# Retention, low-rank mixing and MLP on one core: q, k, v loaded as float32 by SP's queue in a fixed order, and mixing that ends at nine tenths of the MLP beside it

## The chip, the cores and the metric

One core of one Trainium2 chip. The metric is device time in microseconds (us). Most runs of one kernel agree within about 1%. The record marks each run as fast or slow. The medians here are over all runs. The traces are of one profiled execution each. A trace's span is about 2 us shorter than the time of its run, and can differ by more from the median where slow runs are in it.

The engines are TensorE (PE in the profile), VectorE (DVE), ScalarE (ACT), GpSimd (POOL) and SyncE (SP), which here only issues DMA transfers. The granted clock is the share of TensorE's full clock that the chip allowed.

## The reference, cut to what matters

```python
# q, k, v: (8, 8, 576, 64) float32
scores = scale * q @ k^T                          # per batch and head
ret = scores * gamma**(i - j) for i >= j          # causal decay
x = (ret @ v), heads side by side: (8, 576, 512)
h = (x^T @ U @ V)^T                               # mixing over the sequence, rank 32
u = x + h
out = u + max(u @ w_ch1, 0) @ w_ch2               # MLP, 512 -> 2048 -> 512
```

## The kernel before

Two batches are packed into nine chunks of 128 rows. Chunks 0 to 4 make an "A" group (its MLP covers 4 chunks), chunks 5 to 8 a "B" group (its MLP covers 5, since chunk 4 is shared). There are eight groups. While TensorE works through the MLP of group g ("main"), the attention and mixing of group g+1 ("fill") are woven between its matmuls, and the loads of group g+2 are under way.

```python
def interleave(main, fill, lead=0.0, end=1.0):    # fill spread over lead..end of main
    ...

def load_chunk(p, c, cast_dma):
    t = qkv_pool.tile([P, 3, H, D], BF16, tag="qkv", name="qkv")
    if cast_dma:                                  # groups 2 to 7
        for j, dram in ((1, k), (0, q), (2, v)):
            for rows, b, t0 in parts(p, c):
                nc.gpsimd.dma_start(out=t[rows, j, :, :], in_=dram[...])   # f32 -> bf16
        scale_v(t, t, p, c)                       # POOL: v times decay
        return t
    ...                                           # groups 0 and 1: f32 by nc.sync

def attention_items(p, chunks, st, pe_transpose, lag):
    def T(c):                                     # q, k to qkT, crossbar transpose
        nc.sync.dma_start_transpose(out=qkT, in_=t[:, 0:2, :, :]...)
    def SC(c):                                    # scores into psc
        ...
        if c == XC:                               # the shared chunk
            nc.gpsimd.tensor_copy(out=qT[:, :, 0:HALF], in_=qkT[...])      # qTx, POOL
        ...
        nc.vector.tensor_tensor(out=ret, in0=psc, in1=mask, op=ALU.mult)   # DVE
    def RV(c):                                    # ret @ v into po, then xt on DVE
        ...

def mixer_items(p, par, st, pe_transpose):
    def MT(c):                                    # u to uT, input of the next MLP
        nc.sync.dma_start_transpose(out=dst, in_=st["u", c])
    ...

with tc.manual_schedule(engines={PE, POOL}):      # these two in program order
    ...
    for g, (p, par) in enumerate(groups):
        if g + 2 < len(groups):
            load_group(*groups[g + 2])
        fill = front_items(*groups[g + 1]) if g + 1 < len(groups) else []
        interleave(mlp_items(p, par, sts[p]), fill, 0.35 if g == 0 else 0.0)
```

TensorE and POOL run in program order. The order of the other engines, and of SP's DMA queue, is chosen by the scheduler at compile time. Each engine then executes its own list strictly in order.

Of the kernel before, what the change touches and what calls it, by code (L numbers as in the profile page):

```python
# [12 lines left out]
ALU = mybir.AluOpType  # L13
PE = mybir.EngineType.PE
POOL = mybir.EngineType.Pool


def interleave(main, fill, lead=0.0, end=1.0):


    tm = sum(c for c, _ in main) or 1
    tf = sum(c for c, _ in fill) or 1
    i = j = 0
    dm = df = 0.0
    while i < len(main) or j < len(fill):
        if j >= len(fill) or (
            i < len(main) and dm / tm <= lead + (end - lead) * df / tf
        ):
            dm += main[i][0]
            main[i][1]()  # L30
            i += 1
        else:
            df += fill[j][0]
            fill[j][1]()
            j += 1
# [3 lines left out]
def kernel(  # L39
# [11 lines left out]
    nc = tc.nc  # L51

    B, H, S, D = q.shape
# [3 lines left out]
    P = 128  # L57
    HALF = 64
# [7 lines left out]
    XC = 4  # L66
# [31 lines left out]
    vscale = consts.tile([P, NCH, H], FP32, name="vscale")  # L98
# [7 lines left out]
    vx = [consts.tile([P, H, D], BF16, name=f"vx{i}") for i in range(2)]  # L106
# [67 lines left out]
    def parts(p, c):  # L174

        if c < XC:
            return [(slice(0, P), 2 * p, c * P)]
        if c > XC:
            return [(slice(0, P), 2 * p + 1, c * P - 4 * P - HALF)]
        return [(slice(0, HALF), 2 * p, 4 * P), (slice(HALF, P), 2 * p + 1, 0)]  # L180

    def scale_v(t, f, p, c):
        nc.gpsimd.tensor_tensor(  # L183
            out=t[:, 2, :, :], in0=f[:, 2, :, :],
            in1=vscale[:, c, :, None].to_broadcast([P, H, D]), op=ALU.mult,
        )
        if c == XC:
            nc.gpsimd.tensor_copy(out=vx[p % 2][HALF:P, :, :], in_=t[HALF:P, 2, :, :])


    def load_chunk(p, c, cast_dma):
        t = qkv_pool.tile([P, 3, H, D], BF16, tag="qkv", name="qkv")
        if cast_dma:
            for j, dram in ((1, k), (0, q), (2, v)):
                for rows, b, t0 in parts(p, c):
                    L = rows.stop - rows.start
                    nc.gpsimd.dma_start(  # L197
                        out=t[rows, j, :, :],
                        in_=dram[b, :, t0:t0 + L, :].rearrange("h s d -> s h d"),
                    )  # L200
            scale_v(t, t, p, c)
            return t
        f = stage.tile([P, 3, H, D], FP32, tag="stage", name="stage_t")
        for j, dram in ((1, k), (0, q), (2, v)):
            for rows, b, t0 in parts(p, c):
                L = rows.stop - rows.start
                nc.sync.dma_start(  # L207
                    out=f[rows, j, :, :],
                    in_=dram[b, :, t0:t0 + L, :].rearrange("h s d -> s h d"),
                )  # L210
        nc.vector.tensor_copy(out=t[:, 0:2, :, :], in_=f[:, 0:2, :, :])  # L211
        scale_v(t, f, p, c)
        return t


    def attention_items(p, chunks, st, pe_transpose, lag):
        items = []
        qkv = st["qkv"]

        def T(c):  # L220
            t = qkv[c]
# [98 lines left out]
        def add(fn, c, w):  # L320
            items.append((w, lambda: fn(c)))
# [9 lines left out]
        n = len(chunks)  # L331
        if chunks[0] == XC + 1:
            add(ST, XC, 230)
        for s in range(n + lag):
            if s < n:
                add(T, chunks[s], 460 if pe_transpose else 0)
            if lag and s >= lag:
                add(RV, chunks[s - lag], 232)
            if s < n:
                c = chunks[s]  # L340
                if c not in (XC, NCH - 1):
                    add(ST, c, 230)
                add(SC, c, 520)
                if not lag:
                    if c > 0:
                        add(MA0, c - 1, 216)
                    add(RV, c, 232)
        if not lag:
            add(MA0, chunks[-1], 216)
        return items  # L350


    def mixer_items(p, par, st, pe_transpose):
        items = []
        Ub, Vb = (U_A, V_A) if par == 0 else (U_B, V_B)
        c0 = 0 if par == 0 else XC

        def MA(i):
            if pe_transpose:
                pass  # L360
            elif i == 0:
                st["a"] = ps_s.tile([P, dm], FP32, tag="ps_s", name="psa")
            if not pe_transpose:
                nc.tensor.matmul(  # L364
                    st["a"], Ub[:, i, :], st["x", c0 + i], start=(i == 0), stop=(i == 4),
                )
            if i == 4:
                a_sb = mix_pool.tile([P, dm], BF16, tag=f"a_sb{par}", name="a_sb")
                nc.scalar.activation(out=a_sb, in_=st["a"], func=AF.Copy)  # L369
                st["a_sb", par] = a_sb  # L370

        def MH(c):
            if c % 2 == 0:
                ph = ps_s.tile([P, dm], FP32, tag="ps_s", name="ph")
            else:
                ph = ps_o.tile([P, 2, 512], FP32, tag="ps_o", name="ph")[:, 0, :]
            i = c - c0
            if c == XC:
                nc.tensor.matmul(
                    ph, V_A[:, 4 * P:5 * P], st["a_sb", 0], start=True, stop=False  # L380
                )
            nc.tensor.matmul(  # L382
                ph, Vb[:, i * P:(i + 1) * P], st["a_sb", par],
                start=(c != XC), stop=True,
            )
            ut = u_pool.tile([P, dm], BF16, tag="u", name="ut")
            st["u", c] = ut
            nc.vector.tensor_tensor(out=ut, in0=ph, in1=st["x", c], op=ALU.add)  # L388

        def MT(c):  # L390
            dst = st["uT", par][:, :, (c - c0) * P:(c - c0 + 1) * P]
            if not pe_transpose:
                nc.sync.dma_start_transpose(out=dst, in_=st["u", c])  # L393
                return
            pu = ps_big.tile([P, NCC, P], BF16, tag="ps_big", name="pu")
            for cc in range(NCC):
                nc.tensor.transpose(
                    pu[:, cc, :], st["u", c][:, cc * P:(cc + 1) * P], ident
                )
            nc.scalar.activation(out=dst, in_=pu, func=AF.Copy)  # L400

        def start():
            n = 4 if par == 0 else 5
            st["uT", par] = uT_pool.tile([P, NCC, n * P], BF16, tag=f"uT{par}", name="uT")

        for i in range(5):
            items.append((216, lambda i=i: MA(i)))
        items.append((0, start))
        for c in range(c0, c0 + (4 if par == 0 else 5)):
            items.append((216, lambda c=c: MH(c)))  # L410
            items.append((230 if pe_transpose else 0, lambda c=c: MT(c)))
        return items
# [48 lines left out]
    NP = B // 2  # L461
    sts = [{"qkv": {}} for _ in range(NP)]
    A_CH = list(range(0, XC + 1))
    B_CH = list(range(XC + 1, NCH))

    def load_group(p, par, cast_dma=True):
        for c in A_CH if par == 0 else B_CH:
            sts[p]["qkv"][c] = load_chunk(p, c, cast_dma)

    def front_items(p, par, pe_t=False, lag=1):  # L470
        st = sts[p]
        return attention_items(
            p, A_CH if par == 0 else B_CH, st, pe_t, lag
        ) + mixer_items(p, par, st, pe_t)

    with tc.manual_schedule(engines={PE, POOL}):
        early_consts()
        for c in A_CH:
            sts[0]["qkv"][c] = load_chunk(0, c, False)
            if c == 1:  # L480
                load_mixer()
            if c == 3:
                load_w1([0])
        interleave([], front_items(0, 0, True, 0))
        load_w1(range(1, dff // W1B))
        load_w2()
        load_group(0, 1, False)
        groups = [(p, par) for p in range(NP) for par in range(2)]
        for g, (p, par) in enumerate(groups):
            if g + 2 < len(groups):  # L490
                load_group(*groups[g + 2])
            fill = front_items(*groups[g + 1]) if g + 1 < len(groups) else []
            interleave(mlp_items(p, par, sts[p]), fill, 0.35 if g == 0 else 0.0)


# [28 lines left out]
```

## Time and profile before

| | before |
|---|---|
| median of 3 runs | 409.43 us (408.39 to 411.16) |
| span of the trace | 410.2 us |
| first MLP matmul | 42.2 us |
| mean granted TensorE clock | 0.929 |
| length of the eight groups, us | 66.1, 47.5, 40.2, 46.2, 38.9, 51.2, 37.0, 41.0 |

The length of a group runs from its first MLP matmul to the next group's first, in the timeline of TensorE; the last one runs to the end of the span. The page, engines and DMA queues (packets, megabytes, share of 16 engines):

```profile
PE 329.0 (80%) x2406; PEld 179.1 (44%) x2440; DVE 126.0 (31%) x172; ACT 123.5 (30%) x244; POOL 137.4 (33%) x176
...
q0 software_dynamic: 90176, 14.97, 49.1%
q1 hardware_dynamic: 83456, 28.85, 35.2%
```

TensorE leads, but is idle for a fifth of the span. Where it waits, in the view of waits (total us, times, longest us):

```profile
PE ps_y_940 L429 <- DMA uT<-ut: 21.0, 1, 21.0
...
PE psc L265 <- DMA qkT<-qkv: 6.1, 1, 6.1
...
PE ps_y_2783 L429 <- DMA uT<-ut: 4.0, 1, 4.0
PE ps_y_1469 L429 <- DMA uT<-ut: 3.5, 1, 3.5
PE ps_y_2383 L429 <- DMA uT<-ut: 3.4, 1, 3.4
```

L429 is the first MLP layer: every joint, the passage from one group to the next, waits for uT, the transposed output of the mixing, and the first joint waits 21 us. The timeline of SP's queue shows why (start us, us, what):

```profile
82.79 1.23 SPq L225 DMA_TRANSPOSE qkT<-qkv  x1
84.12 0.53 SPq L447 DMA_DIRECT2D out_dram<-o_sb  x1
89.93 1.23 SPq L225 DMA_TRANSPOSE qkT<-qkv  x1
91.22 0.57 SPq L447 DMA_DIRECT2D out_dram<-o_sb  x1
97.01 1.23 SPq L225 DMA_TRANSPOSE qkT<-qkv  x1
98.34 0.52 SPq L447 DMA_DIRECT2D out_dram<-o_sb  x1
98.95 5.34 SPq L393 DMA_TRANSPOSE uT<-ut  x4
104.40 0.53 SPq L447 DMA_DIRECT2D out_dram<-o_sb  x1
105.47 1.19 SPq L393 DMA_TRANSPOSE uT<-ut  x1
```

The mixing's matmuls ended at 87.3 us, but the uT transposes (L393) start at 98.95. In front of them stand attention transposes of the third group (L225) at 7.1 us intervals. They wait for POOL's cast loads, whose timeline is:

```profile
76.39 1.04 POOL L183 TENSOR_TENSOR qkv<-qkv,vscale 128x512 bf16<-128x512 bf16 x1 [3.53 <-DMA qkv<-in_v_dram]
77.38 0.94 POOL L197 DMA_DIRECT2D qkv<-in_k_dram  x1
78.31 0.89 POOL L197 DMA_DIRECT2D qkv<-in_q_dram  x1
79.18 0.90 POOL L197 DMA_DIRECT2D qkv<-in_v_dram  x1
83.58 1.04 POOL L183 TENSOR_TENSOR qkv<-qkv,vscale 128x512 bf16<-128x512 bf16 x1 [3.50 <-DMA qkv<-in_v_dram]
```

POOL issues a chunk's three loads, waits 3.5 us for them, scales v, and only then issues the next chunk: 7.2 us per chunk. A long wait also costs clock. The windows view of TensorE (length, busy us, matmuls, granted clock, DMA share, GB/s):

```profile
85.00:90.00 5.00, 2.25 (x10) 0.95 1.40 140
90.00:95.00 5.00, 0.00 (x0) 0.50 0.89 135
...
105.00:110.00 5.00, 1.65 (x8) 0.50 1.65 179
110.00:115.00 5.00, 4.80 (x30) 0.66 1.36 106
```

After the wait the matmuls go on at half clock for some microseconds.

### The profile page before, as it was taken

Reading aid. Unit: us, or ns where it says so; the run is one execution under the profiler, and the core shown is the slowest. Engines: PE = TensorE matmul, PEld = TensorE weight load, DVE = VectorE, ACT = ScalarE, POOL = GpSimd, SP = SyncE. Lnnn points to the kernel's source line nnn. Section 1 sums busy time; section 2 is a strip of 40 time slices with the busy share of each in tenths; the row PEclk is TensorE's granted clock in tenths of the full one; section 3 lists DMA queues with packets and bytes.
Section 4 is the critical chain, followed back from the end, with each engine's and each line's share of the span. In section 5 each row is a group of like instructions: output and inputs, shape, how many; then the busy total and the mean of one; then the engine's idle time right before and its main releaser. Section 6 shows DMA issues by size and latency. Waiting matters only on the chain.

```text
span 410.2 us, 5915 instructions
## 1 busy us (share of the span) xinstructions
PE 329.0 (80%) x2406; PEld 179.1 (44%) x2440; DVE 126.0 (31%) x172; ACT 123.5 (30%) x244; POOL 137.4 (33%) x176
## 2 busy tenths in 40 slices
PE   2554948950499987997899969993999979988995
PEld 1442414420276433543675434541675435435642
DVE  4445003440033341334134323431324323350021
ACT  3222542000166003610572015301571026105700
POOL 2835805457336436533643426333100000000000
PEclk9999987985599996999899989996899989999999
DMA  9999999999999999999999949999120220031011
GB/s 182 202 204 182 205 180 134 95 120 138 149 90 93 100 189 108 91 127 132 126 93 100 144 108 90 102 123 144 27 53 27 88 67 0 27 90 53 0 53 77
DMA packets 173659, 44.19 MB, mean 108 GB/s; under 512 B 164864, under 2 KB 169024, under 8 KB 173632
## 3 DMA queue, kind: packets, MB, share of 16 engines
q0 software_dynamic: 90176, 14.97, 49.1%
q1 hardware_dynamic: 83456, 28.85, 35.2%
q8 instruction: 19, 0.31, 0.3%
q14 instruction: 8, 0.07, 0.1%
HBM read 37.00 MB, written 9.44 MB: 113 GB/s over the span
## 4 chain that ended last, share of the span: by engine, by line
PE 67%; DMA 11%; issue 8%; POOL 7%; SPq 3%; DVE 2%; ACT 1%; POOLq 0%; DVEq 0%
DMA uT<-ut 6%; POOL qkv L197 3%; PE psc L265 3%; POOL qkv L183 2%; DMA w_sb<-in_moe_w_ch_dram 2%; PE po L305 2%; SPq L393 2%; PE psa L364 2%; PE pss L248 1%; POOL w_sb L169 1%; PE ph L382 1%; DMA stage_t<-in_v_dram 1%; DMA U_A<-in_moe_U_dram 1%; SPq L207 1%; PE ps_y_3231 L440 1%
## 5 line engine op out<-in xcount | busy, mean ns | idle before, releaser
L429 PEld LDWEIGHTS <-w_sb 128*128 128x128 bf16 x768 | 74.4, 103 | 96.0 <-issue 38.0
L292 DVE TENSOR_TENSOR ret<-psc,tri 128x1024 bf16<-128x1024 f32 x32 | 39.2, 1224 | 107.9 <-PE psc L265 107.9
L183 POOL TENSOR_TENSOR qkv<-qkv,vscale 128x512 bf16<-128x512 bf16 x27 | 28.0, 1037 | 111.1 <-DMA qkv<-in_v_dram 111.1
L311 DVE TENSOR_TENSOR xt<-po,qscale 128x512 bf16<-128x512 f32 x36 | 24.9, 690 | 53.0 <-PE po L305 53.0
L388 DVE TENSOR_TENSOR ut<-ph,xt 128x512 bf16<-128x512 f32 x36 | 24.8, 690 | 27.1 <-PE ph L382 25.9
L369 ACT ACTIVATE a_sb<-psa 128x512 bf16<-128x512 f32 x8 | 4.8, 597 | 85.8 <-PE psa L364 81.8
L197 POOL DMA_DIRECT2D qkv<-in_k_dram x30 | 26.9, 899 | 7.9 <-PE pss L248 7.9
L197 POOL DMA_DIRECT2D qkv<-in_v_dram x30 | 25.9, 869 | 0.0
L197 POOL DMA_DIRECT2D qkv<-in_q_dram x30 | 25.6, 857 | 0.0
L265 PE MATMUL psc<-qkT 64*128 64x128 bf16 x288 | 16.0, 238 | 9.4 <-DMA qkT<-qkv 6.1
L305 PE MATMUL po<-qkv,ret 128*128 128x64 bf16 x288 | 15.4, 200 | 6.5 <-DVE ret L292 4.6
L255 ACT ACTIVATE s_sb<-pss 128x512 bf16<-128x512 f32 x32 | 19.0, 593 | 4.1 <-PE pss L248 3.9
L305 PEld LDWEIGHTS <-ret 128*128 128x128 bf16 x288 | 13.7, 102 | 12.5 <-DVE ret L292 6.8
L265 PEld LDWEIGHTS <-qkT 64*128 64x128 bf16 x288 | 9.1, 101 | 22.5 <-issue 11.5
L429 PE MATMUL ps_y_940<-uT,w_sb 128*128 128x320 bf16 x4 | 1.2, 459 | 21.0 <-DMA uT<-ut 21.0
L183 POOL TENSOR_TENSOR qkv<-stage_t,vscale 128x512 bf16<-128x512 f32 x9 | 9.3, 1046 | 21.8 <-DMA stage_t<-in_v_dram 17.6
L248 PEld LDWEIGHTS <-qkv 128*128 128x128 bf16 x128 | 11.9, 115 | 8.1 <-issue 3.0
L248 PE MATMUL pss<-qkv 128*128 128x128 bf16 x112 | 13.0, 249 | 1.6 <-ACT s_sb L255 1.0
L211 DVE CAST qkv<-stage_t 128x1024 bf16<-128x1024 f32 x9 | 6.3, 702 | 22.1 <-DMA stage_t<-in_q_dram 22.1
L440 PEld LDWEIGHTS <-y_3632 128*128 128x128 bf16 x80 | 7.8, 98 | 9.3
L440 PEld LDWEIGHTS <-y_2767 128*128 128x128 bf16 x80 | 7.6, 98 | 8.6
L440 PEld LDWEIGHTS <-y_939 128*128 128x128 bf16 x80 | 7.6, 98 | 8.6
(526 smaller groups left out, 568.9 us busy)
## 6 DMA issues: line engine op xcount, KB each, us to landing
out_dram<-o_sb SPq DMA_DIRECT2D x36, 256.0 KB, 2.3
qkv<-in_k_dram POOLq DMA_DIRECT2D x24, 128.0 KB, 3.6
qkv<-in_q_dram POOLq DMA_DIRECT2D x24, 128.0 KB, 4.6
qkv<-in_v_dram POOLq DMA_DIRECT2D x24, 128.0 KB, 4.6
stage_t<-in_k_dram SPq DMA_DIRECT2D x8, 256.0 KB, 5.8
stage_t<-in_q_dram SPq DMA_DIRECT2D x8, 256.0 KB, 5.3
stage_t<-in_v_dram SPq DMA_DIRECT2D x8, 256.0 KB, 5.5
w_sb<-in_moe_w_ch_dram POOLq DMA_DIRECT2D x16, 128.0 KB, 7.0
```

The source lines that it names most:

```text
L183: nc.gpsimd.tensor_tensor(out=t[:, 2, :, :], in0=f[:, 2, :, :], in1=vscale[:, c, :, None].to_broadcast([P, H, D]), op=ALU.mult,)
L197: nc.gpsimd.dma_start(out=t[rows, j, :, :], in_=dram[b, :, t0:t0 + L, :].rearrange("h s d -> s h d"),)
L248: nc.tensor.matmul(pss[:, hp, :], t[:, 1, 2 * hp:2 * hp + 2, :].rearrange("p h d -> p (h d)"), vt[:, 2 * hp:2 * hp + 2, :].rearrange("p h ...
L255: nc.scalar.activation(out=s_sb, in_=pss, func=AF.Copy)
L265: nc.tensor.matmul(psc[:, hl, hp, :], qkT[pb:pb + HALF, NHP + hp, :], qkT[pb:pb + HALF, hp, :], start=True, stop=True,)
L292: nc.vector.tensor_tensor(out=ret.rearrange("p (hp hl) i -> p hl hp i", hl=2), in0=psc, in1=mask[:, None, None, :].to_broadcast([P, 2, NHP ...
L305: nc.tensor.matmul(po[:, hl, hp * D:(hp + 1) * D], ret[:, h, :], t[:, 2, h, :], start=(c == 0 and hp == 0), stop=True, skip_group_check=True,)
L311: nc.vector.tensor_tensor(out=xt.rearrange("p (hp hl d) -> p hl hp d", hl=2, d=D), in0=po[:, :, 0:NHP * D].rearrange("p hl (hp d) -> p hl ...
L364: nc.tensor.matmul(st["a"], Ub[:, i, :], st["x", c0 + i], start=(i == 0), stop=(i == 4),)
L388: nc.vector.tensor_tensor(out=ut, in0=ph, in1=st["x", c], op=ALU.add)
L429: nc.tensor.matmul(ps[:, 0:n], w1_sb[:, cc, f * P:(f + 1) * P], uT[:, cc, t0:t0 + n], start=(cc == 0), stop=(cc == NCC - 1),)
L440: nc.tensor.matmul(ps, st["y1"][:, f, i * P:(i + 1) * P], w2_sb[:, f, :], start=(f == 0), stop=(f == NF - 1),)
```

## The change

Three things are changed together:
- **L, loads.** All q, k, v come as float32 through SP's queue. The cast of q and k moves to DVE. A load can then be issued without POOL.
- **O, order.** SP joins the engines in program order. Each attention transpose is placed one step ahead of its use, each chunk's load after it (before, a group's loads all stood at the start of an MLP).
- **M, mixing.** The fill runs from 0.05 to 0.9 of the MLP in place of 0 to 1, so that uT has time to land.

```diff
-        if cast_dma:
-            ... nc.gpsimd.dma_start(out=t[rows, j, :, :], in_=dram[...])
-            scale_v(t, t, p, c)
-            return t
         f = stage.tile([P, 3, H, D], FP32, tag="stage", name="stage_t")
         ... nc.sync.dma_start(out=f[rows, j, :, :], in_=dram[...])
         nc.vector.tensor_copy(out=t[:, 0:2, :, :], in_=f[:, 0:2, :, :])
...
+        if not pe_transpose:
+            add(T, chunks[0], 0)
         for s in range(n + lag):
-            if s < n:
-                add(T, chunks[s], 460 if pe_transpose else 0)
+            if pe_transpose and s < n:
+                add(T, chunks[s], 460)
+            if not pe_transpose and s + 1 < n:
+                add(T, chunks[s + 1], 0)
+            if loads:
+                items.append((0, lambda a=loads.pop(0): load_chunk(*a)))
...
-    with tc.manual_schedule(engines={PE, POOL}):
+    with tc.manual_schedule(engines={PE, POOL, SPQ}):
...
-            interleave(mlp_items(p, par, sts[p]), fill, 0.35 if g == 0 else 0.0)
+            interleave(main, fill, 0.35 if g == 0 else 0.05, 0.9)
```

More of the change, by code (lines that the diff above doesn't have):

```diff
@@ L15 @@
 POOL = mybir.EngineType.Pool
+SPQ = mybir.EngineType.SP
 def interleave(main, fill, lead=0.0, end=1.0):
@@ L180, in parts, with load_chunk @@
         return [(slice(0, HALF), 2 * p, 4 * P), (slice(HALF, P), 2 * p + 1, 0)]
-    def scale_v(t, f, p, c):
-        nc.gpsimd.tensor_tensor(
-            out=t[:, 2, :, :], in0=f[:, 2, :, :],
-            in1=vscale[:, c, :, None].to_broadcast([P, H, D]), op=ALU.mult,
-        )
-        if c == XC:
-            nc.gpsimd.tensor_copy(out=vx[p % 2][HALF:P, :, :], in_=t[HALF:P, 2, :, :])
-    def load_chunk(p, c, cast_dma):
-        t = qkv_pool.tile([P, 3, H, D], BF16, tag="qkv", name="qkv")
-        if cast_dma:
-            for j, dram in ((1, k), (0, q), (2, v)):
-                for rows, b, t0 in parts(p, c):
-                    L = rows.stop - rows.start
-                    nc.gpsimd.dma_start(
-                        out=t[rows, j, :, :],
-                        in_=dram[b, :, t0:t0 + L, :].rearrange("h s d -> s h d"),
-                    )
-            scale_v(t, t, p, c)
-            return t
+    def load_chunk(p, c):
+        t = qkv_pool.tile([P, 3, H, D], BF16, tag="qkv", name="qkv")
         f = stage.tile([P, 3, H, D], FP32, tag="stage", name="stage_t")
@@ L211, in load_chunk, with attention_items @@
         nc.vector.tensor_copy(out=t[:, 0:2, :, :], in_=f[:, 0:2, :, :])
-        scale_v(t, f, p, c)
-        return t
-    def attention_items(p, chunks, st, pe_transpose, lag):
+        nc.gpsimd.tensor_tensor(
+            out=t[:, 2, :, :], in0=f[:, 2, :, :],
+            in1=vscale[:, c, :, None].to_broadcast([P, H, D]), op=ALU.mult,
+        )
+        if c == XC:
+            nc.gpsimd.tensor_copy(out=vx[p % 2][HALF:P, :, :], in_=t[HALF:P, 2, :, :])
+        sts[p]["qkv"][c] = t
+    def attention_items(p, chunks, st, pe_transpose, lag, loads):
         items = []
         qkv = st["qkv"]
+        loads = list(loads)
         def T(c):
@@ L349, in attention_items @@
             add(MA0, chunks[-1], 216)
+        for a in loads:
+            items.append((0, lambda a=a: load_chunk(*a)))
         return items
@@ L464, with chunks_of, front_items @@
     B_CH = list(range(XC + 1, NCH))
-    def load_group(p, par, cast_dma=True):
-        for c in A_CH if par == 0 else B_CH:
-            sts[p]["qkv"][c] = load_chunk(p, c, cast_dma)
-    def front_items(p, par, pe_t=False, lag=1):
-        st = sts[p]
+    def chunks_of(g):
+        return [(g // 2, c) for c in (A_CH if g % 2 == 0 else B_CH)] if g < 2 * NP else []
+    def front_items(g, loads, pe_t=False, lag=1):
+        p, par = g // 2, g % 2
         return attention_items(
-            p, A_CH if par == 0 else B_CH, st, pe_t, lag
-        ) + mixer_items(p, par, st, pe_t)
-    with tc.manual_schedule(engines={PE, POOL}):
+            p, A_CH if par == 0 else B_CH, sts[p], pe_t, lag, loads
+        ) + mixer_items(p, par, sts[p], pe_t)
+    with tc.manual_schedule(engines={PE, POOL, SPQ}):
         early_consts()
         for c in A_CH:
-            sts[0]["qkv"][c] = load_chunk(0, c, False)
+            load_chunk(0, c)
             if c == 1:
@@ L483 @@
                 load_w1([0])
-        interleave([], front_items(0, 0, True, 0))
+        interleave([], front_items(0, [], True, 0))
         load_w1(range(1, dff // W1B))
         load_w2()
-        load_group(0, 1, False)
-        groups = [(p, par) for p in range(NP) for par in range(2)]
-        for g, (p, par) in enumerate(groups):
-            if g + 2 < len(groups):
-                load_group(*groups[g + 2])
-            fill = front_items(*groups[g + 1]) if g + 1 < len(groups) else []
-            interleave(mlp_items(p, par, sts[p]), fill, 0.35 if g == 0 else 0.0)
+        for a in chunks_of(1):
+            load_chunk(*a)
+        for g in range(2 * NP):
+            main = mlp_items(g // 2, g % 2, sts[g // 2])
+            fill = front_items(g + 1, chunks_of(g + 2)) if g + 1 < 2 * NP else []
+            interleave(main, fill, 0.35 if g == 0 else 0.05, 0.9)
 _INS = ['q', 'k', 'v', 'moe_U', 'moe_V', 'moe_w_ch1', 'moe_w_ch2']
```

## The prediction

> **What bounds the kernel now.** TensorE, with holes. The windows view in 5 us stretches shows it busy nearly 5 of 5 us inside most groups (one MLP of 4 or 5 chunks, with the next group's attention and mixing beside it) and idle at the joints between them. From the first MLP matmul (42 us) to the end I count about 75 us lost:
> - First joint, 87 to 108 us: one wait of 21.0 us for the transposed mixing output (waits view: ps_y_940 on DMA uT). In the SP queue's timeline that transpose stands behind two attention transposes, which wait for cast loads. Those go chunk by chunk: the chain of waits alternates a 1.04 us POOL scale, 2.65 us of issuing and 3.5 us of landing, 7.2 us per chunk.
> - Six later joints: waits of 2.8 to 8 us for uT.
> - After long waits the granted clock falls. The Trainium skill, "TensorE: Matmul & The Clock Gate" (What's actually happening), puts this at about 3.4 us idle. The trace agrees: 0.50 at 155 to 160 us after a gap of 3.5 us, 1.00 after the last joint's waits of 1.3 and 1.9 us. Gaps plus slow clock: about 61 us.
> - In the first group about 9 us, one attention transpose stuck behind weight traffic (psc on qkT, 6.1 us).
>
> **What the change does.** It removes 90 cast issues from POOL (0.87 us each, 78 us), adds 90 hardware issues on SP (0.5 us when free, 1.1 when full, as in the first 20 us) and 27 DVE casts of 0.69 us. POOL scales cost the same; TensorE's work is unchanged. A chunk's load should take 3.6 us (five in 18 us at the start), against 7.2. SP's order is now fixed: uT transposes no longer stand behind later attention transposes, and each attention transpose is queued one step ahead. Mixing ends at 0.9 of the MLP, so 16 matmuls (3.45 us) follow each group's last mixing matmul.
>
> **On the critical path.** The 21 us wait should vanish almost wholly. At other joints, after the last mixing matmul: 1.1 us (DVE), an output issue (0.5), one or two transposes (1.3 each), 3 us from issue to landing; this ends about 2 us after the 3.45 us of matmuls. Each of seven joints keeps about 2 us, mostly too short for the clock to fall: 17 us in place of 61. The first group's hole stays, 3 to 4 us worse: DVE casts the third group's first chunk before the first masking, and that load queues behind two transposes. Loads crowding SP in groups with five loads: 2 us.
>
> 410 - 61 + 17 + 4 + 2: about **371 us**, 8 in 10 between **360** and **387**. Faster by over 2%: 0.96; within 2%: 0.03; slower: 0.01.
>
> **What the profile would show.**
> - Software queue: weights and mixer only; POOL busy near 50 us; DVE near 145.
> - First joint's wait for uT under 4 us; the others 1 to 3; mean clock from 0.93 to 0.96 or more.
> - First MLP matmul still near 42 us; first qkT wait still 6 us or more.
> - After the first group no waits over 2 us for qkT.
>
> **What would make it wrong.** SP is in order: transposes behind three loads in a full queue (one took 10.6 us to issue before) could make TensorE wait for qkT in every group: 385 to 395. DVE is in order too: a cast ahead of a masking, whose load is late, holds TensorE. If uT lands earlier than I count, the joints vanish: 358.

## The result, and the profile after

| | before | changed |
|---|---|---|
| median of 4 runs | 410.3 us | 381.35 us (380.06 to 383.07) |
| ratio | | 0.9289, 95% interval 0.9215 to 0.9363 |
| span of the trace | 410.2 us | 381.3 us |
| first MLP matmul | 42.2 us | 41.8 us |
| mean granted clock | 0.929 | 0.978 |
| groups, us | 66.1, 47.5, 40.2, 46.2, 38.9, 51.2, 37.0, 41.0 | 51.3, 49.9, 35.2, 46.0, 37.1, 45.2, 35.1, 39.8 |

A ratio is the mean time of one kernel's fast runs over that of the other's fast runs of the same rounds, so it is not quite the ratio of the medians. Line numbers move with the edit: L393 of before is L390 here, L225 is L214, L429 is L426.

The page of the changed kernel:

```profile
PE 329.2 (86%) x2440; PEld 176.1 (46%) x2440; DVE 142.9 (37%) x199; ACT 123.2 (32%) x244; POOL 62.4 (16%) x86
...
q1 hardware_dynamic: 167840, 50.09, 73.6%
q0 software_dynamic: 5792, 4.34, 7.5%
```

Waits of TensorE:

```profile
PE po L294 <- DVE ret L281: 9.6, 10, 2.6
...
PE psc L254 <- DMA qkT<-qkv: 5.7, 2, 4.6
...
PE ps_y_936 L426 <- DMA uT<-ut: 1.9, 1, 1.9
PE ps_y_2800 L426 <- DMA uT<-ut: 1.6, 1, 1.6
```

The 21 us are gone. The first joint waits 0.8 and 1.9 us, the other joints 0.6 to 1.6 us. SP's queue at the first joint:

```profile
83.88 0.57 SPq L444 DMA_DIRECT2D out_dram<-o_sb  x1
86.91 2.53 SPq L390 DMA_TRANSPOSE uT<-ut  x2
89.96 0.35 SPq L444 DMA_DIRECT2D out_dram<-o_sb  x1
90.37 3.85 SPq L390 DMA_TRANSPOSE uT<-ut  x3
94.31 0.53 SPq L444 DMA_DIRECT2D out_dram<-o_sb  x1
```

No attention transpose stands in front of uT any more. The saving of 28.9 us (410.2 less 381.3) is unevenly spread. The first group gives 14.9. The third to eighth give 16.0 together, the start 0.4. The second became 2.3 us longer. The new first line of the waits tells of it: TensorE waits for the masking on DVE (ret). Here is DVE in the second group,

```profile
113.79 0.68 DVE L300 TENSOR_TENSOR xt<-po,qscale 128x512 bf16<-128x512 f32 x1
119.22 0.69 DVE L194 CAST qkv<-stage_t 128x1024 bf16<-128x1024 f32 x1 [4.75 <-DMA stage_t<-in_q_dram]
119.83 1.22 DVE L281 TENSOR_TENSOR ret<-psc,tri 128x1024 bf16<-128x1024 f32 x1
```

and TensorE beside it:

```profile
115.89 0.40 PE L254 MATMUL psc<-qkT 64*128 64x128 bf16 x8
...
121.11 0.41 PE L294 MATMUL po<-qkv,ret 128*128 128x64 bf16 x8 [2.64 <-DVE ret L281]
```

The scores were in psc at 116.3 us. DVE could have masked them then, but stood at the cast of a chunk that is needed only in a later group, whose load had not landed. The clock then fell:

```profile
115.00:120.00 5.00, 3.47 (x36) 1.00 1.06 184
120.00:125.00 5.00, 3.89 (x33) 0.72 0.00 0
```

### The profile page after: what moved, and what is told of

Same layout as the page of the kernel before. It is cut to its first block, busy times and chain, and to the rows that moved or that the text cites. A ratio compares the mean times of both kernels' runs of the same rounds, so it can differ in the third digit from the quotient of the medians.

```text
span 381.3 us, 5987 instructions
## 1 busy us (share of the span) xinstructions
PE 329.2 (86%) x2440; PEld 176.1 (46%) x2440; DVE 142.9 (37%) x199; ACT 123.2 (32%) x244; POOL 62.4 (16%) x86
## 3 DMA queue, kind: packets, MB, share of 16 engines
q0 software_dynamic: 5792, 4.34, 7.5%
## 4 chain that ended last, share of the span: by engine, by line
PE 56%; DMA 18%; SPq 13%; DVE 6%; issue 3%; ACT 2%; POOL 1%; DVEq 0%; POOLq 0%
DMA stage_t<-in_q_dram 8%; SPq L190 7%; DMA uT<-ut 4%; SPq L214 4%; DMA stage_t<-in_v_dram 3%; DVE ret L281 3%; PE po L294 2%; PE psc L254 2%; PE psa L361 2%; PE ph L379 1%; SPq L390 1%; DVE o_sb L443 1%; DVE qkv L194 1%; DMA qkT<-qkv 1%; DMA U_A<-in_moe_U_dram 1%
## 5 line engine op out<-in xcount | busy, mean ns | idle before, releaser
L426 PEld LDWEIGHTS <-w_sb 128*128 128x128 bf16 x768 | 72.2, 100 | 55.9 <-issue 17.3
L195 POOL TENSOR_TENSOR qkv<-stage_t,vscale 128x512 bf16<-128x512 f32 x36 | 38.1, 1060 | 216.2 <-DMA stage_t<-in_v_dram 156.0
L194 DVE CAST qkv<-stage_t 128x1024 bf16<-128x1024 f32 x36 | 25.8, 718 | 64.4 <-DMA stage_t<-in_q_dram 64.4
L237 PEld LDWEIGHTS <-qkv 128*128 128x128 bf16 x128 | 10.5, 105 | 6.9 <-issue 1.9
L237 PE MATMUL pss<-qkv 128*128 128x128 bf16 x112 | 12.0, 235 | 1.8 <-ACT s_sb L244 1.0
L437 PEld LDWEIGHTS <-y_3686 128*128 128x128 bf16 x80 | 7.8, 98 | 9.3
L437 PEld LDWEIGHTS <-y_929 128*128 128x128 bf16 x80 | 7.8, 101 | 9.3 <-issue 1.1
L437 PEld LDWEIGHTS <-y_1861 128*128 128x128 bf16 x80 | 7.6, 98 | 8.6
L437 PEld LDWEIGHTS <-y_2793 128*128 128x128 bf16 x80 | 7.6, 98 | 8.6
L221 PE MATMUL pst<-ident,qkv 128*128 128x128 bf16 x40 | 5.2, 311 | 7.3 <-DVE qkv L194 7.3
L226 ACT ACTIVATE qkT<-pst 128x1024 bf16<-128x1024 bf16 x5 | 5.1, 1024 | 15.1 <-PE pst L221 15.1
L163 POOL DMA_DIRECT2D w_sb<-in_moe_w_ch_dram x16 | 9.3, 597 | 3.5 <-DMA w_sb<-in_moe_w_ch_dram 3.5
L437 PEld LDWEIGHTS <-y_1457 128*128 128x128 bf16 x64 | 6.1, 98 | 7.1
```

Source lines behind the costliest of these rows:

```text
L194: nc.vector.tensor_copy(out=t[:, 0:2, :, :], in_=f[:, 0:2, :, :])
L195: nc.gpsimd.tensor_tensor(out=t[:, 2, :, :], in0=f[:, 2, :, :], in1=vscale[:, c, :, None].to_broadcast([P, H, D]), op=ALU.mult,)
L237: nc.tensor.matmul(pss[:, hp, :], t[:, 1, 2 * hp:2 * hp + 2, :].rearrange("p h d -> p (h d)"), vt[:, 2 * hp:2 * hp + 2, :].rearrange("p h ...
L426: nc.tensor.matmul(ps[:, 0:n], w1_sb[:, cc, f * P:(f + 1) * P], uT[:, cc, t0:t0 + n], start=(cc == 0), stop=(cc == NCC - 1),)
L437: nc.tensor.matmul(ps, st["y1"][:, f, i * P:(i + 1) * P], w2_sb[:, f, :], start=(f == 0), stop=(f == NF - 1),)
```

## The experiments

The changed kernel's theory was: the 21 us wait is the order of SP's queue, the other joints are the time left for uT, and what remains is DVE's order and a hole in the first group. Its rivals: the rate of the cast loads is what counts; or only one of the three parts is needed.

### One or two parts of the change at a time

**e1, L and O without M** (the changed kernel, fill over the whole MLP):

```diff
-            interleave(main, fill, 0.35 if g == 0 else 0.05, 0.9)
+            interleave(main, fill, 0.35 if g == 0 else 0.0)
```

> The changed kernel with the mixing spread over the whole MLP again, as before (lead 0, end 1.0): hardware loads and fixed queue order stay. If ending the mixing at 0.9 is what shortened the later joints, their waits for uT return to 2.5 to 3.5 us with slow clock after them, and the time is 390 to 398 us. If the joints were shortened by the lighter DMA traffic alone, the waits stay under 2 us and the time is within 3 us of the changed kernel (381).

Measured: 404.92 us, ratio to before 0.9859 (0.9813 to 0.9904). The waits for uT return, and the mean clock falls to 0.932:

```profile
PE ps_y L426 <- DMA uT<-ut: 30.8, 11, 4.2
```

So without M most of the gain is lost (404.9 against 381.4 us), and the time is within 2% of the kernel before. This was expected, but the loss is larger than expected (390 to 398 us). The wait of 21 us does not return: the first joint waits 2.9 and 2.3 us. So L and O remove it without M. The other joints wait 25.6 us together, against 23.4 before.

**e2, M alone** (the kernel before, fill from 0.05 to 0.9):

```diff
-            interleave(mlp_items(p, par, sts[p]), fill, 0.35 if g == 0 else 0.0)
+            interleave(mlp_items(p, par, sts[p]), fill, 0.35 if g == 0 else 0.05, 0.9)
```

> The kernel before with only the mixing moved (lead 0.05, end 0.9): cast loads and the scheduler's own SP order. The compiled SP order still has attention transposes of the third group, which wait for cast loads, ahead of the first joint's uT transposes. So the first joint's wait shrinks (the matmuls come earlier but the queue is still blocked), to 5 to 15 us; later joints drop under 2 us. 385 to 397 us. If it comes to 381 or less, the loads and the order were worth nothing.

Measured: 399.56 us, ratio 0.9723 (0.9681 to 0.9764). The first joint still waits 18.6 us, more than the 5 to 15 expected: the mixing is done earlier, but its transposes still stand behind three attention transposes, the last of them issued at 97.00 us (97.01 before). The time is above the expected 385 to 397, and the later joints keep single waits of up to 3.3 us in place of under 2. Ending early helps only where the queue is free to use it.

**e3, O and M without L** (cast loads on POOL, SP in program order):

```diff
-    with tc.manual_schedule(engines={PE, POOL}):
+    with tc.manual_schedule(engines={PE, POOL, SPQ}):
...
+            if not pe_transpose and s + 1 < n:
+                add(T, chunks[s + 1], 0)
...
+            interleave(mlp_items(...), fill, 0.35 if g == 0 else 0.05, 0.9)
```

> The kernel before with cast loads kept on POOL, but SP's order fixed, attention transposes one step ahead, and mixing ending at 0.9: all of the change but the hardware loads. Theory A (the 21 us wait was the queue's order): first joint under 4 us, 378 to 390 us, so the hardware loads are worth little or nothing. Theory B (it was the rate of cast loads, 7.2 us per chunk): the wait comes back as PE waiting for qkT in the second and third groups, 395 us or more.

Measured: 410.49 us against 411.76 for before, with runs from 405.71 to 414.16, two of the four slow (the fast ones are 405.71 and 408.69), and no interval: no gain shown. Neither theory had it right. The loads on POOL still stand at the start of each MLP here, as before. The first joint's gap did shrink to 3.2 us, as theory A said. But a new wait appeared in the second group, not for qkT as theory B said:

```profile
119.11 0.40 PE L266 MATMUL psc<-qkT 64*128 64x128 bf16 x8
135.43 0.40 PE L285 MATMUL po<-s_sb,qTx 64*128 64x64 bf16 x8 [15.92 <-POOL qTx L279]
```

POOL's timeline of e3 at that place:

```profile
133.99 1.04 POOL L184 TENSOR_TENSOR qkv<-qkv,vscale 128x512 bf16<-128x512 bf16 x1 [3.24 <-DMA qkv<-in_v_dram]
134.98 0.39 POOL L279 COPY qTx<-qkT 128x256 bf16<-128x256 bf16 x1
```

A copy of 0.39 us stood behind the scales of four cast loads that POOL issues and waits for in order. The wait had only moved from SP's queue to POOL's.

**e5, e3 with that copy on DVE:**

```diff
-                    nc.gpsimd.tensor_copy(
+                    nc.vector.tensor_copy(
                         out=qT[:, :, 0:HALF], in_=qkT[:, 0:NHP, 0:HALF]
```

> Run e3 (cast loads, fixed SP order, mixing end 0.9) with the one small copy of the transposed queries of the shared chunk moved from POOL to DVE. In e3 TensorE waited 15.9 us for that copy, which stood on POOL behind the scales of four cast loads. If POOL's order is the cause, that wait vanishes and the time is 386 to 396 us (e3 410, less 16 us and the slow clock after it, joints still slower than in the changed kernel under cast traffic). If the cast loads are too slow in themselves (7.2 us per chunk), TensorE waits for qkT instead and the time stays over 400.

Measured: 389.71 us, ratio 0.9499 (0.9449 to 0.9549), inside the expected range. The 15.9 us wait is gone, and no wait for qkT over 2.9 us came in its place. So the rate of the cast loads is not the limit; two in-order queues were. What e5 loses against the changed kernel is at the joints (waits for uT of 22.1 us in all against 8.1), while its first group is shorter (44.3 us against 51.3): e5's second group ends with a 4.2 us gap, its uT transpose issued at 135.02 us and the next MLP starting at 141.10. In the changed kernel the same transpose is issued at 140.33 and the MLP starts at 142.88. The transposes themselves land later in the kernels with cast loads: the longest takes 6.5 to 7.4 us in all four of them, and 2.7 to 4.3 in all ten with hardware loads. Why is not shown. Issue to landing (min, median, max) in the kernel before,

```profile
DMA to landing us min/median/max: 2.4/2.9/6.6
```

in e5,

```profile
DMA to landing us min/median/max: 2.4/2.8/6.5
```

and in the changed kernel:

```profile
DMA to landing us min/median/max: 2.4/2.5/4.0
```

**e8, L and M without the fixed order** (the changed kernel, SP's order left to the scheduler; the places of transposes and loads in the program stay new):

```diff
-    with tc.manual_schedule(engines={PE, POOL, SPQ}):
+    with tc.manual_schedule(engines={PE, POOL}):
```

> The changed kernel without the fixed SP order: hardware loads, mixing end 0.9, but SP's order left to the scheduler. The compiled order puts parts of the next loads between the uT transposes from the second joint on. If the fixed order is needed beside hardware loads, the uT waits at the joints from the second on grow to 3 to 5 us each with slow clock, and the time is 388 to 396 us. If it isn't, 379 to 384.

Measured: 375.21 us, ratio 0.9168 (0.9105 to 0.9231). A clear miss: the joints did not get worse, uT landed within 3.2 us at most, and the time is, if anything, shorter. The changed kernel run again, **e11**, on a chip of the same number gave 381.52 us and 0.9221 (0.9159 to 0.9284); the intervals overlap, so e8 is not shown to be faster, only not slower.

> The changed kernel again, on the chip of e9 and e10, to compare with them and with e4 and e8: 379 to 383 us as before, ratio to before 0.92 to 0.935.

What e8 tests has to be read from SP's queue:

```profile
84.50 2.52 SPq L390 DMA_TRANSPOSE uT<-ut  x2
92.55 2.65 SPq L214 DMA_TRANSPOSE qkT<-qkv  x2
...
127.73 1.28 SPq L214 DMA_TRANSPOSE qkT<-qkv  x1
...
131.69 2.50 SPq L390 DMA_TRANSPOSE uT<-ut  x2
```

At the first joint the scheduler chose the fixed order by itself: uT goes out before the third group's attention transposes. So e8 does not test whether the order matters for the wait of 21 us. At the second joint it put all four attention transposes of the fourth group (113.81 to 127.73 us) in front of uT, and TensorE waits only 0.66 us there. So, with hardware loads, attention transposes that stand early need not hold the queue. The parts together (no run has L alone or O alone):

| loads | SP order | mixing ends | run | median us | ratio to before | longest wait after the first group's hole |
|---|---|---|---|---|---|---|
| cast | free | 1.0 | before | 410.3 | 1 | first uT, 21.0 us |
| cast | free | 0.9 | e2 | 399.6 | 0.972 | first uT, 18.6 us |
| cast | fixed | 0.9 | e3 | 410.5 | none given | POOL's copy, 15.9 us |
| cast | fixed | 0.9 | e5, copy on DVE | 389.7 | 0.950 | uT at joints, up to 5.7 us |
| hardware | fixed | 1.0 | e1 | 404.9 | 0.986 | uT at joints, up to 4.2 us |
| hardware | fixed | 0.9 | changed | 381.4 | 0.929 | ret on DVE, up to 2.6 us |
| hardware | free, new places | 0.9 | e8 | 375.2 | 0.917 | uT at joints, up to 2.1 us |

### What was left: DVE's order

**e4, casts later.** DVE in program order too, with each chunk's cast and POOL scale two steps after its load:

```diff
-    with tc.manual_schedule(engines={PE, POOL, SPQ}):
+    with tc.manual_schedule(engines={PE, POOL, SPQ, DVE}):
...
+            if s >= 2 and casts:
+                items.append((0, lambda a=casts.pop(0): convert(*a)))   # cast and scale
...
-                items.append((0, lambda a=loads.pop(0): load_chunk(*a)))
+                items.append((0, lambda a=loads.pop(0): load_chunk(*a, False)))  # DMA only
```

> The changed kernel with DVE's order fixed too, and each chunk's DVE cast and POOL scale placed two steps after its load. If the cast standing too early in DVE's order is what held TensorE (11 us of PE waits for ret, 2.6 us of it before the long slow patch of the second group), those waits drop below 4 us in total, the second group takes 44 to 46 us in place of 49.8, and the time is 372 to 377 us. If the late loads themselves are the limit, the waits move to qkT or POOL and the time stays at 381.

Measured: 374.46 us, ratio 0.9114 (0.9078 to 0.9149). The second group takes 43.7 us in place of 49.9, and TensorE waits for ret nowhere in it; the total of such waits (4.6 us) missed the 4 that were expected by little. The late loads were not the limit: a cast that comes later in DVE's list waits for nothing. Cast and scale were moved together, and DVE's whole order was fixed with them, so their shares are not separated. The hole in the first group was not touched, and is longer here (window 40 to 93 us):

```profile
PE psc L268 <- DMA qkT<-qkv: 7.2, 1, 7.2
```

### What was left: the hole in the first group

All three next kernels start from e4. **e6** issues three of the second group's transposes between its loads instead of after them:

```diff
         for i, a in enumerate(chunks_of(1)):
             load_chunk(*a)
             cast_chunk(*a)
+            if i >= 1:
+                ... nc.sync.dma_start_transpose(...)      # qkT of the chunk before
```

> Run e4 (casts later, 374.5 us) with the first three attention transposes of the second group issued between that group's four loads instead of after them. If the hole in the first group (7.2 us wait for qkT and slow clock after it) comes from the transpose standing behind loads in SP's full queue, it closes to under 2 us and the time is 364 to 369 us. If it comes from the weights filling the DMA engines, the transpose lands as late as before and the time stays at 374.

Measured: 379.28 us (372.61, then 379.12 to 379.73, these three slow; no interval, so nothing is claimed from the time). In the trace the wait for qkT is gone, and a wait of 7.1 us for ret has taken its place; the first group takes 52.6 us, as in e4 (52.7). DVE stood at a cast whose load landed at 61.9 us.

**e7** issues the second weight after the second group's q, k, v:

```diff
-        load_w2()
         for a in chunks_of(1):
             load_chunk(*a)
             cast_chunk(*a)
+        load_w2()
```

> Run e4 with the second weight's loads issued after the second group's q, k, v loads. If weight traffic is what delays the first qkT, it lands 5 us or more earlier; but the second weight then arrives later, and TensorE may wait for it at the first output matmuls (68 us). Queue theory: qkT earlier by 3 us at most, since SP's order is unchanged. Time 368 to 378 us, sign open.

Measured: 377.95 us, ratio 0.9189 (0.9121 to 0.9257). The wait for qkT falls to 1.8 us, and TensorE waits 5.3 us for the weight instead. The first group takes 56.9 us.

**e9** is e6 with two casts moved back, so that DVE's order cannot be the cause:

```diff
-            cast_chunk(*a)
+            if i < 3:
+                cast_chunk(*a)
...
+            if p == 0 and chunks[0] == XC + 1 and s == 2:
+                items.append((0, lambda: cast_chunk(0, NCH - 1)))
...  # and the fifth cast of a five-chunk load goes to the end of the mixing
```

> Run e6 with two more casts moved: the last chunk of the second group is cast after the second masking instead of before the first, and the last chunk of each five-chunk load is cast after the mixing. In e6 the 7.2 us wait for qkT had become a 7.1 us wait for the masking (ret), which stood on DVE behind that cast. If DVE's order is now the only cause of the hole, PE waits for ret fall under 3 us there, the first group takes 43 to 46 us in place of 52.6, and the time is 4 to 8 us under the changed kernel's best variant: 364 to 370 us. If the DMA engines are simply full until 60 us, the wait moves to another tile and the time stays at 372 to 379.

Measured: 371.4 us, ratio 0.8986 (0.8936 to 0.9037). Faster than the changed kernel of the same rounds (381.52), but not through the hole: the first group still takes 52.6 us. The wait moved a third time: TensorE waits 5.6 us for ret, behind the cast of the third chunk, which waits for its load:

```profile
60.58 0.69 DVE L202 CAST qkv<-stage_t 128x1024 bf16<-128x1024 f32 x1 [20.35 <-DMA stage_t<-in_q_dram]
```

Four orders (e4, e6, e7, e9) moved the wait from qkT to ret, to the weight and to ret behind another cast, and the first group stayed as long or grew. That points to the bytes and away from the order. **e12** takes bytes away: e4 with one of the eight loads of the second weight, the other blocks zeroed on DVE; its result is wrong.

```diff
         for f in range(0, NF, 2):
+            if f >= 2:
+                nc.vector.memset(w2_sb[:, f:f + 2, :], 0.0)
+                continue
             nc.gpsimd.dma_start(
```

> Run e4 with only one of the eight loads of the second weight; the other seven blocks are zeroed on DVE, so the result is wrong on purpose. This takes about 3.7 MB of weight reads off the DMA engines between 40 and 60 us and changes no queue's order. If those bytes are what holds the first group's qkT (7.2 us in e4), that wait falls under 2 us, the first group takes 37 to 43 us in place of 52.7, and the time is 360 to 366 us. If SP's order is the cause, the wait stays over 5 us and the time at 374.

Measured: 364.92 us, ratio 0.8896 (0.8843 to 0.895). No wait for qkT is left in the first group, which takes 43.3 us in place of 52.7; the second to the seventh group differ from e4 by at most 0.3 us. So the hole comes from the weights and nine chunks of q, k, v passing the same DMA engines until about 60 us (193 GB/s over the first 60 us in both the kernel before and the changed one). e12 also takes seven issues off POOL and adds work to DVE, but the way from load to qkT has no step on POOL: SP has issued its last chunk load by 47.3 us in place of 54.8.

The order is not without effect, though. e5 moves all these bytes too, and its first group takes 44.3 us; with hardware loads and all the bytes it takes 48.6 (e8) to 56.9 (e7). Most of the weights are issued from 25.7 us on there (29.6 in the changed kernel), since they no longer stand behind a copy on POOL; TensorE waits 2.9 us for qkT; and little waits behind it. In e4 the mixing waits another 2.9 us at 86.3 us, because DVE stands at a cast of the third group. No run joins e5's start to hardware loads.

**e10** is e9 with the mixing ending at 0.85:

> e9 with the mixing ending at 0.85 of the MLP. If the remaining waits for uT at the joints (8 us in all in e4 and e6) are only the tail of one or two transposes, about 1.5 us more room per joint removes most of them: 3 to 6 us under e9. If crowding the front costs as much in waits for ret and qkT, the same time as e9 within 2 us.

Measured: 371.54 us, ratio 0.8972 (0.8912 to 0.9031): the same as e9. The waits for uT fell from 7.4 to 6.4 us only. e9 is the version to keep: its ratio to the changed kernel, from the two ratios of the same rounds, is 0.8986 / 0.9221 = 0.975.

## Why the prediction was right or wrong, point by point

The time lay inside the range (381.35 in 360 to 387), 10 us above the centre of 371.

- **"The 21 us wait should vanish almost wholly": right.** It became 0.8 and 1.9 us.
- **The reason given for it, "SP's order is now fixed: uT transposes no longer stand behind later attention transposes": supported, but not the whole.** The 21.0 and 18.6 us stand only where attention transposes go in front of the first uT (before, e2). With cast loads the fixed order removes that wait (e3, 3.2 us left), but another in-order queue, POOL's, brings 15.9 us back. With hardware loads the order need not be fixed by hand (e8), since the scheduler chose the same one at this joint. Whether hardware loads alone would have cured it, with the old order, no run shows.
- **"At other joints ... about 2 us": right in size,** 0.6 to 1.6 us. That M is what does it was right too (e1).
- **"Mostly too short for the clock to fall": right** for six of seven joints; at the first the clock fell to 0.67 over 95 to 100 us.
- **"The first group's hole stays, 3 to 4 us worse": right in kind, more in size,** here read from the trace by subtraction: the first group without the wait that ends it took 45.1 us before (66.1 less 21.0) and 50.4 after (51.3 less 0.8), so 5.3 us worse. The wait for qkT alone was 4.6 us, under the 6 that the prediction asked for; a wait of 1.4 us for ret came behind it.
- **"No waits over 2 us for qkT" after the first group: right,** the only one is 1.0 us.
- **DVE's order outside the first group was named as a risk and not priced: this term of the sum failed.** It made the second group 49.9 us; with the casts later it takes 43.7 (e4), 6.2 us that the sum does not have.
- **The joints were over-counted on both sides.** An estimate by lengths of groups: groups with hardly a wait take 35.1 us (A, the seventh of the changed kernel) and 42.5 us (B, the sixth of e8), and the last one 39.8 us (the changed kernel). Four A, three B, the last and a start of 42 come to 140.4 + 127.5 + 39.8 + 42 = 349.7 us. So the kernel before lost about 60 us after its start, not 75, and the changed kernel loses 381.3 - 349.7 = 31.6 us, near the 36 that the prediction left it (371 less 335). Without the first group's hole (10.0 and 15.3 us over the 35.1) and the 6.2 us of DVE, the joints cost about 50 us before, in place of 61, and 10 after, in place of 17. They saved 40 in place of 44.
- **So the 10 us to the centre are** about 6 for DVE, which e4 shows (its median is 6.9 us under the changed kernel's), and about 4 for the joints, which is an estimate; the hole's 5.3 stand against 4 + 2 in the sum. That the errors on the joints nearly cancel is luck. How much of the 61 was never there depends on the count. The waits for uT are 44.4 us in the kernel before, and in the half-clock stretches from the first joint on TensorE was busy for 25.4 us, of which the clock can have cost at most half: 57 us by this estimate.
- Smaller readings: POOL fell to 62.4 us, not 50; DVE rose to 142.9 (145 said); the mean clock to 0.978 (0.96 or more said); the software queue carries 4.34 MB.

## What to carry to other kernels

When a queue that runs in order holds an item that waits for a late load, everything behind it is late, and fixing one such queue can hand the wait to the next one (SP to POOL in e3, SP to DVE in e6 and e9). So look for what makes the item wait before you re-order, and place work for a later stage behind the work that the current stage needs. To tell an order problem from a shortage of bandwidth, take bytes away (e12). Then still look for a run with all the bytes and a shorter stage (e5): both can limit it.

## What the Trainium skill lacked or had wrong

- "TensorE: Matmul & The Clock Gate" (What's actually happening) gives about 3.4 us of idle for the clock to fall. Here the matmuls stopped for 2.64 us in the changed kernel's second group and the clock over the next 5 us was 0.72 (0.50 from 122.2 to 125.6 us); a wait of 2.60 us in e4 (at 256 us) left the matmuls at full speed. The runs show that a gap of 2.6 us may or may not cost clock.
- "DMA: Bandwidth & Descriptors" (SWDGE vs HWDGE vs iDMA) says that a cast during DMA is for POOL's software queue only. The kernel before does it so, and no run tried another queue. The runs show the price that the page does not give: with the scale of v on the same engine, 7.2 us per chunk of q, k, v, during which POOL can do nothing that stands behind it. The cast on DVE costs 718 ns per chunk in the changed kernel.
- The same page (Issuing engines are not separate DMA queues) says that DMAs of all issuing engines interleave on the same 16 DMA engines. With seven weight loads of POOL's queue gone, SP issues its last chunk load by 47.3 us in place of 54.8 (e12 and e4). But no page says that a DMA transpose lands later in a kernel with cast loads: up to 6.6 us before and 6.5 in e5, up to 4.0 in the changed kernel, for the same 32 uT transposes.
- No page says how long SP can be held at issuing one load when the DMA engines are busy: 6.31 us at 40.3 us in the changed kernel, against 0.45 us for the first load of the run.
